# Two steps of the expert taken together from the 33rd step on, with a retuned table of orders

## The chip, the cores and the metric

The kernel runs on one core of one Trainium2 chip. The metric is the device time of one execution in microseconds (us); times of several executions are given by their median. The engines of the core are TensorE (PE in the rows, with PEld for its weight loads), VectorE (DVE), ScalarE (ACT), GpSimd (POOL) and SyncE (SP, which here issues all transfers).

## What is computed

Three parts follow each other, on 4 batches of 768 tokens, 8 heads of 48 values (d_model 384):

```python
# 1. attention with a decaying state, per head
for t in range(S):
    cur = einsum('bhd,bhe->bhde', u[None] * k[t], v[t])
    y[:, :, t] = einsum('bhd,bhde->bhe', r[t], state + cur)
    state = w[t][..., None] * state + einsum('bhd,bhe->bhde', k[t], v[t])
# 2. the first expert, x = y as [3072, 384]
h = x @ w_in                              # [3072, 2048]
g = h * clip(h + 3, 0, 6) / 6
x = g @ w_out                             # [3072, 384]
# 3. eight experts with four soft slots each
logits = x @ phi                          # [3072, 32]
d = softmax of logits over the tokens     # dispatch
slot_input = d.T @ x                      # [32, 384]
slot_out[e] = relu(slot_input[e] @ w1[e]) @ w2[e]
out = softmax of logits over the slots @ slot_out
```

w_in and w_out come as 64-bit floats and are turned into 32-bit ones in the kernel.

## The kernel before

The 3072 tokens are cut into 24 chunks g of 128 tokens (a batch has six), and three chunks make a block m of 384 tokens; there are eight blocks. The attention works chunk by chunk, the first expert block by block. One block goes through 16 steps of the expert, one for each 128 columns of w_in, so there are 128 steps s = 16 m + f in all.

One step is `moe_h` (L490): nine matmuls L498 (three pieces of d_model, each as three products of high and low parts) add up h of 384 tokens in a PSUM bank of the pool `ps_h`. The pool has NH = 3 banks, so the matmuls of step s + 3 can't start before step s has given its bank back. ScalarE's L501 computes the clipped part from the bank, VectorE's L502 multiplies it with the bank into the tile g (eight buffers); with L502 the bank is free. Two steps later `moe_t` (L521) turns g: for the middle blocks with VectorE's L529 and two transfers through memory (`moe_v`, L518 and L519), for the first two blocks and the end on TensorE (L222). `moe_l` multiplies four finished g with the product of w_out and phi (L551), which gives the logits. When a block's logits are complete, `r_logits` adds them up: ScalarE's L570 and VectorE's L571 split them into `part`, TensorE's L573 sums, and L583 to L646 make the running softmax and add the block into `acc` (L643, L646). After step 127 the tail does part 3.

For each chunk of the attention there are the loads (`wkr` L234, three buffers; `rkv` L243, two), the scan L250 on VectorE that makes `e` and ScalarE's small copy L254 of it, the second scan L260, the products L263 (with `e`, `pk`), L270 (`pq`), L276 (`rk`) and L280 (`ru`), each on VectorE or GpSimd by the tables PKD, PQD, RKD and RUD, the row sums L284, the diagonal of `att` (four of ScalarE's L293 or one of GpSimd's L295 by the table DGA, for two halves), the squares L267, the scores on TensorE (L306) and VectorE's masked copies L311 of them, the products L373 and L377, the copies L394 and L395 into y, and the state L333, L348, L349. A block's three y go through a transfer (L400), and ScalarE's L419 and GpSimd's or VectorE's L420 split them into the high and low part of x, which `moe_h` reads.

What sets the order: the program is a list of tokens (`seq`). A token is one of these pieces for one chunk, step or block (`pw19` the first scan of chunk 19, `h68` the matmuls, L501 and L502 of step 68, `o66` the turning of step 66). The start is written out by hand (START). After it each token of the attention has a step, worked out from its chunk's block (YB) and moved by the table LATER; at each step come first the tokens A, B, C (the splitting of w_in), then `h`, then the turning of two steps before, then the logits and then all other tokens of that step. The order of `seq` is the order of priority; a scheduler that simulates the engines makes each engine's order from it. Each engine then runs its instructions in that order, and an instruction that waits holds those behind it.

Of the kernel before, what the change touches and what calls it, by code (L numbers as in the profile page):

```python
# [29 lines left out]
NF = DFF // 128  # L30
# [134 lines left out]
def emit(ctx, tc, wkr, rkv, u, wi, wo, wot, phi, w1, w2, consts, out, flag=None, ysc=None):  # L165
    nc = tc.nc
    LAG = 2
# [735 lines left out]
    with ExitStack():  # L903
# [109 lines left out]
        seq = []  # L1013
# [54 lines left out]
        for s in sorted(set(steps) | set(range(NF * NB + LAG))):  # L1068
            early = [t for t in steps.get(s, ()) if t[0] in "ABC"]
            seq += early  # L1070
            if 0 <= s < NF * NB:
                seq.append(f"h{s}")
            late = [t for t in steps.get(s, ()) if t[0] not in "ABC"]
            if s >= LAG:
                seq.append(f"o{s - LAG}")
                if (s - LAG) % 4 == 3:
                    seq.append(f"v{(s - LAG) // 4}")
            seq += [t for t in late if t[0] == "l"]
            seq += [t for t in late if t[0] != "l"]
            if s == OPEN:  # L1080
                seq.append("open")
# [41 lines left out]
MT = 2  # L1123
QEND = 30
# [107 lines left out]
```

## Time and profile before

| | us |
|---|---|
| three executions, median | 535.35 (534.69 to 539.89) |
| the profiled execution | 535.26 |
| its span, first to last instruction | 533.5 |
| TensorE busy | 474.5 (89%) |
| VectorE busy | 366.4 (69%) |
| ScalarE busy | 237.5 (45%) |
| GpSimd busy | 153.0 (29%) |

The span is a little shorter than the execution, 1.8 us lie around it. The expert's matmuls L498 alone are 232.2 us of TensorE's work, L501 is 71.9 us of ScalarE's, L502 68.7 us of VectorE's. In a row of the order in time the number in front is the start, the next one the duration, both in us; in square brackets stands for how long the engine stood still just before the first instruction of the row, and what ended that. A row of several equal instructions (x9) runs from the first start to the last end.

### The profile page before, as it was taken

To read this page: it belongs to the slowest core of one execution; us is meant where nothing else is said; L and a number is where in the kernel's file an instruction comes from. 1 tells how busy PE (TensorE), PEld (TensorE's weight loads), DVE (VectorE), ACT (ScalarE), POOL (GpSimd) and SP (SyncE) were. 2 spreads that over 40 slices of the span, in tenths; PEclk is the share of its full clock that TensorE was granted. 3 is DMA by queue.
4 is the path that set the end of the run, shared out by engine and by line. 5 is a ranking of instruction groups with operands and counts; after the bars stand their busy time and mean duration, and the time that the engine had idled before them with its cause. 6 is when DMAs were issued, how large, how long until landed. Compare 5 with 4: busy or idle time off the path is not lost.

```text
span 533.5 us, 10165 instructions
## 1 busy us (share of the span) xinstructions
PE 474.5 (89%) x3934; PEld 375.0 (70%) x3934; DVE 366.4 (69%) x669; ACT 237.5 (45%) x580; POOL 153.0 (29%) x150
## 2 busy tenths in 40 slices
PE   5866786999999999999999997998999999989992
PEld 5755675688877688787875774886788788753462
DVE  5899999588425577798795799679667667442241
ACT  3574666477454343535362446245224323341021
POOL 3556932515101142233261643335130010000000
PEclk9687896698989999999999999999999999999995
DMA  8974235722303043668748965967496999977957
GB/s 297 413 280 123 88 122 183 259 86 70 107 3 109 1 121 109 184 192 279 268 120 249 326 224 145 286 222 197 119 329 199 377 315 336 419 324 270 398 172 232
DMA packets 40263, 114.13 MB, mean 214 GB/s; under 512 B 4464, under 2 KB 22928, under 8 KB 40208
## 3 DMA queue, kind: packets, MB, share of 16 engines
q1 hardware_dynamic: 40208, 113.41, 63.0%
q8 instruction: 33, 0.54, 0.4%
q14 instruction: 22, 0.18, 0.1%
HBM read 90.34 MB, written 22.02 MB: 211 GB/s over the span
## 4 chain that ended last, share of the span: by engine, by line
PE 45%; DVE 15%; DMA 9%; ACT 4%; issue 2%; POOL 2%; SPq 1%; POOLq 0%; DVEq 0%; ACTq 0%
PE h L498 22%; DMA rkv<-in_rkv_dram 4%; DMA wkr<-in_wkr_dram 4%; PE lps L551 3%; PE rot L222 3%; PE sides L643 3%; DVE g L502 2%; DVE wkr L260 2%; PE rot L799 2%; DVE e L250 2%; PE rot L373 2%; DVE gsq L529 2%; PE rot L377 2%; PE sides L306 1%; PE po L851 1%
## 5 line engine op out<-in xcount | busy, mean ns | idle before, releaser
L498 PE MATMUL h<-x,wt 128*128 128x384 f32 x1152 | 232.2, 349 | 21.6 <-DVE g L502 11.0
L498 PEld LDWEIGHTS h<-x,wt 128*128 128x128 f32 x1152 | 201.1, 192 | 43.6 <-DVE g L502 15.0
L501 ACT ACTIVATE g<-h,half 128x384 f32<-128x384 f32 x128 | 71.9, 575 | 62.6 <-PE h L498 57.7
L502 DVE SCALAR_TENSOR_TENSOR g<-g,h 128x384 f32<-128x384 f32 x128 | 68.7, 542 | 39.6 <-ACT g L501 36.0
L529 DVE STREAM_TRANSPOSE gsq<-g 128x384 f32<-128x384 f32 x88 | 49.6, 569 | 4.1 <-DMA via<-gsq 2.9
L250 DVE TENSOR_TENSOR_SCAN e<-wkr,d1r 128x516 f32<-128x516 f32 x24 | 32.3, 1351 | 23.2 <-DMA wkr<-in_wkr_dram 23.1
L295 POOL TENSOR_TENSOR att<-cst,cd 128x512 f32<-128x512 f32 x32 | 37.0, 1169 | 27.1 <-DVE cd L284 21.7
L270 POOL TENSOR_TENSOR wkr<-wkr 128x512 f32<-128x512 f32 x18 | 23.9, 1328 | 64.3 <-DVE wkr L260 35.9
L311 DVE COPY_PREDICATED att<-upm,sides 128x512 f32<-128x512 uint32 x48 | 32.1, 721 | 11.3 <-POOL att L295 5.7
L377 PE MATMUL rot<-att,rkv 128*64 128x128 f32 x384 | 32.5, 297 | 7.0 <-DVE att L311 7.0
L260 DVE TENSOR_TENSOR_SCAN wkr<-wkr,d1f 128x516 f32<-128x516 f32 x24 | 35.4, 1475 | 0.1
L377 PEld LDWEIGHTS rot<-att,rkv 128*64 128x64 f32 x384 | 25.0, 147 | 13.9 <-DVE att L311 8.2
L306 PE MATMUL sides<-wkr 64*128 64x128 f32 x384 | 31.6, 302 | 3.2 <-DVE wkr L270 1.2
L263 POOL TENSOR_TENSOR wkr<-wkr,e 128x512 f32<-128x512 f32 x16 | 20.9, 1309 | 44.2 <-DVE e L250 38.2
L306 PEld LDWEIGHTS sides<-wkr 64*128 64x128 f32 x384 | 26.0, 202 | 8.5 <-issue 4.3
L551 PE MATMUL lps<-g,ws 128*32 128x384 f32 x256 | 29.2, 519 | 1.2 <-DVE g L502 1.2
L293 ACT ACTIVATE att<-cst,cd 128x128 f32<-128x128 f32 x64 | 20.3, 393 | 16.5 <-DVE cd L284 16.5
L267 ACT ACTIVATE wkr<-wkr 128x516 f32<-128x516 f32 x24 | 15.2, 633 | 26.1 <-POOL wkr L270 15.6
L349 POOL TENSOR_TENSOR st<-sm,pt 128x192 f32<-128x192 f32 x20 | 13.8, 688 | 43.4 <-DVE sm L348 22.3
L280 POOL TENSOR_TENSOR rkv<-rkv,u_b 128x384 f32<-128x384 f32 x18 | 19.5, 1081 | 21.9 <-DVE rkv L276 9.2
L722 POOL COPY c<-chi 128x128 f32<-128x128 f32 x6 | 2.2, 364 | 78.7 <-DVE chi L720 40.9
L373 PE MATMUL rot<-wkr,st 64*64 64x128 f32 x320 | 24.5, 291 | 0.0
(156 smaller groups left out, 664.8 us busy)
## 6 DMA issues: line engine op xcount, KB each, us to landing
piece<-in_w_dram SPq DMA_DIRECT2D x24, 768.0 KB, 7.8
wkr<-in_wkr_dram SPq DMA_DIRECT2D x23, 770.0 KB, 5.2
via<-gsq SPq DMA_DIRECT2D x88, 192.0 KB, 4.4
gnat<-via SPq DMA_DIRECT2D x22, 768.0 KB, 5.9
rkv<-in_rkv_dram SPq DMA_DIRECT2D x24, 640.0 KB, 5.5
wi<-in_wi_dram SPq DMA_DIRECT2D x8, 768.0 KB, 8.9
wo<-in_wo_dram SPq DMA_DIRECT2D x8, 768.0 KB, 4.5
piece<-in_w_dram SPq DMA_DIRECT2D x8, 512.0 KB, 6.9
```

Source lines behind the costliest of these rows:

```text
L250: nc.vector.tensor_tensor_scan(out=flat(e)[:, ::-1], data0=behind.pop(g)[:, ::-1], data1=flat(d1r)[:, ::-1], initial=0.0, op0=ALU.mult, op ...
L260: nc.vector.tensor_tensor_scan(out=fw, data0=fw, data1=fd, initial=0.0, op0=ALU.mult, op1=ALU.add)
L295: nc.gpsimd.tensor_tensor(out=att[g][:, hs, :], in0=ident.unsqueeze(1).to_broadcast([128, 4, C]), in1=cd[g][:, hs].unsqueeze(2).to_broadca ...
L306: nc.tensor.matmul(out=sps[g][:, x, p * C:(p + 1) * C], lhsT=kt_[hs, p, :], rhs=qt_[hs, p, :])
L311: nc.vector.copy_predicated(out=att[g][:, x::2, :], mask=upm.unsqueeze(1).to_broadcast([128, NP, C]), data=ps[:, x].rearrange("p (a t) -> ...
L373: nc.tensor.matmul(out=ps[hs, k * C:(k + 1) * C], lhsT=stl[g][hs, p, :], rhs=qt_[hs, p, :], start=(k == 0), stop=False)
L377: nc.tensor.matmul(out=ps[64 * x:64 * x + 64, k * C:(k + 1) * C], lhsT=vt[:, 2 * p + x, :], rhs=a[:, 2 * p + x, :], start=(first and k == ...
L498: mm = nc.tensor.matmul(out=ps, lhsT=a[:, wp, f % 2, kt * 128:(kt + 1) * 128], rhs=x_[:, xp, kt, :], start=(kt == 0 and i == 0), stop=(kt ...
L501: ra = nc.scalar.activation(out=t, in_=ps, func=ACTF.Relu, scale=1.0 / 6.0, bias=half)
L502: sv = nc.vector.scalar_tensor_tensor(out=t, in0=t, scalar=1.0, in1=ps, op0=ALU.min, op1=ALU.mult)
L529: nc.vector.transpose(out=gsq[m, q][:, :, :, i, :].rearrange("p r j c -> p j r c"), in_=gt[s].rearrange("p (j r c) -> p j r c", j=n, r=4))
L551: mm = nc.tensor.matmul(out=lps[m][32 * i:32 * i + 32, :], lhsT=wsl[q][:, i, :], rhs=gt.pop(NF * m + 4 * q + i), start=(q == 0), stop=(q = ...
```

## The change

From step PAIR = 32 on, two steps are written one right behind the other: first the tokens A, B, C of both, then `h` of both, then for each of the two the turning, the logits and the other tokens. The tables are another set: RKD loses 0, 9 and 23 (to GpSimd), RUD gains 9, 10 and 14, PKD loses 17 and gains 21, PQD gains 11 (to VectorE), DGA gains a half of chunk 6 and one of chunk 19 (to ScalarE). YB puts the first chunk of block 0 one step earlier and the last chunks of blocks 6 and 7 one step later, the first pieces of w_in are loaded and split in another order (PLACES), START has another order, and about half of the numbers in LATER differ.

```diff
-        for s in sorted(set(steps) | set(range(NF * NB + LAG))):
-            early = [t for t in steps.get(s, ()) if t[0] in "ABC"]
-            seq += early
-            if 0 <= s < NF * NB:
-                seq.append(f"h{s}")
-            late = [t for t in steps.get(s, ()) if t[0] not in "ABC"]
-            if s >= LAG:
...
+        order = sorted(set(steps) | set(range(NF * NB + LAG)))
+        k = 0
+        while k < len(order):
+
+            both = order[k:k + 2] if order[k] >= PAIR and order[k] % 2 == 0 else order[k:k + 1]
+            k += len(both)
+            for s in both:
+                seq += [t for t in steps.get(s, ()) if t[0] in "ABC"]
+            seq += [f"h{s}" for s in both if 0 <= s < NF * NB]
+            for s in both:
+                late = [t for t in steps.get(s, ()) if t[0] not in "ABC"]
+                if s >= LAG:
+                    seq.append(f"o{s - LAG}")
+                    if (s - LAG) % 4 == 3:
+                        seq.append(f"v{(s - LAG) // 4}")
+                seq += [t for t in late if t[0] == "l"]
+                seq += [t for t in late if t[0] != "l"]
+                if s == OPEN:
+                    seq.append("open")
...
-RKD = (0, 2, 4, 7, 9, 10, 11, 12, 14, 16, 17, 19, 23)
-RUD = (4, 8, 12, 17, 18, 21)
-PKD = (2, 4, 8, 9, 10, 11, 12, 17)
-PQD = (0, 2, 3, 7, 13, 19)
+RKD = (2, 4, 7, 10, 11, 12, 14, 16, 17, 19)
+RUD = (4, 8, 9, 10, 12, 14, 17, 18, 21)
+PKD = (2, 4, 8, 9, 10, 11, 12, 21)
+PQD = (0, 2, 3, 7, 11, 13, 19)
...
 MT = 2
+PAIR = 32
...
-YB = ((-5, 3, 5), (0, 4, 8), (-6, -2, 4), (-7, -3, 2), (-6, -2, 2), (-10, -8, -1), (-13, -7, -4))
+YB = ((-6, 3, 5), (0, 4, 8), (-6, -2, 4), (-7, -3, 2), (-6, -2, 2), (-10, -8, -1), (-13, -7, -3))
...
-    'W2': 2, 'W3': 3, 'W1': 1, 'W0': 0, 'W4': 1, 'V0': 4, 'V1': 5, 'W5': 4, 'V2': 2, 'V3': 3, 'V4': 5, 'V5': 4, 'W6': 3, 'V6':
+    'W1': 1, 'W3': 3, 'W2': 2, 'W4': 1, 'W0': 0, 'V0': 4, 'V1': 5, 'W5': 4, 'V2': 2, 'V3': 3, 'V4': 5, 'V5': 4, 'W6': 3, 'V6':
```

What this does to an engine's order shows in the following rows. ScalarE before, from L501 of step 65 to that of step 68, where the logits of block 3 are split (`part`, L570); `pt` and `e` are chunk 19's and then chunk 20's:

```order
L501 ACTIVATE g_3081<-h_3071,half_95 128x384
L254 ACTIVATE pt_3126<-e_3123 128x4
L570 ACTIVATE part_3149<-lps_2694 128x384
L267 ACTIVATE e_3123,guard_96<-e_3123 128x516
L501 ACTIVATE g_3139<-h_3129,half_95 128x384
L501 ACTIVATE g_3174<-h_3164,half_95 128x384
L267 ACTIVATE wkr_3069,guard_96<-wkr_3069 128x516
L293 ACTIVATE att_3180<-cst0_91,cd_3146 128x128 x4
L395 ACTIVATE y_2763<-rot_3098 128x3x128
L254 ACTIVATE pt_3332<-e_3329 128x4
L267 ACTIVATE e_3329,guard_96<-e_3329 128x516
L501 ACTIVATE g_3231<-h_3221,half_95 128x384
```

The same place of the change, from `part` on; the three L501 are those of steps 66, 67 and 68:

```order
L570 ACTIVATE part_3165<-lps_2706 128x384
L501 ACTIVATE g_3146<-h_3136,half_95 128x384
L254 ACTIVATE pt_3133<-e_3130 128x4
L501 ACTIVATE g_3159<-h_3149,half_95 128x384
L267 ACTIVATE e_3130,guard_96<-e_3130 128x516
L501 ACTIVATE g_3227<-h_3217,half_95 128x384
L293 ACTIVATE att_3244<-cst0_91,cd_3050 128x128 x4
```

`part` now stands ahead of chunk 19's L254, and L501 of step 68 ahead of the four L293 instead of behind them and three more.

VectorE before, from L502 of step 67 to that of step 68:

```order
L502 SCALAR_TENSOR_TENSOR g_3174<-g_3174,h_3164 128x384
L394 COPY y3_2764<-rot_3098 128x128
L250 SCALAR_TENSOR_TENSOR e_3329<-wkr_3297,d1r_100 128x516
L583 TENSOR_REDUCE mx_3155<-rot_3148 128x1
L529 STREAM_TRANSPOSE gsq_3142<-g_3174 128x3x4x32
L252 RECIPROCAL d1f_99<-e_3329 128x4
L311 COPY_PREDICATED att_3180<-upm_92,sides_3186 128x4x128 x2
L585 TENSOR_TENSOR mrun_104<-mx_3155,mrun_104 128x1
L260 SCALAR_TENSOR_TENSOR wkr_3297<-wkr_3297,d1f_99 128x516
L276 TENSOR_TENSOR rkv_3178<-rkv_3178 128x384
L502 SCALAR_TENSOR_TENSOR g_3231<-g_3231,h_3221 128x384
```

VectorE in the change, from L502 of step 67 to that of step 68 and on to the first scan of chunk 20:

```order
L583 TENSOR_REDUCE mx_3171<-rot_3164 128x1
L502 SCALAR_TENSOR_TENSOR g_3159<-g_3159,h_3149 128x384
L284 TENSOR_REDUCE cd_3050<-rkv_3001 128x8
L270 TENSOR_TENSOR wkr_3048<-wkr_3048 128x512
L585 TENSOR_TENSOR mrun_104<-mx_3171,mrun_104 128x1
L529 STREAM_TRANSPOSE gsq_3162<-g_3159 128x3x4x32
L502 SCALAR_TENSOR_TENSOR g_3227<-g_3227,h_3217 128x384
L250 SCALAR_TENSOR_TENSOR e_3375<-wkr_3283,d1r_100 128x516
```

L502 of step 68 stands ahead of both scans of chunk 20, of the copies L311 and of L276; behind it they follow, mixed with L502 of steps 69 and 70.

ScalarE before around L501 of step 80, where x of block 6 is made (L419):

```order
L254 ACTIVATE pt_3772<-e_3769 128x4
L419 ACTIVATE x_3814<-y_3265 128x384
L254 ACTIVATE pt_3901<-e_3898 128x4
L419 ACTIVATE x_3814<-y_3265 128x384
L267 ACTIVATE e_3769,guard_96<-e_3769 128x516
L501 ACTIVATE g_3648<-h_3638,half_95 128x384
L419 ACTIVATE x_3814<-y_3265 128x384
L501 ACTIVATE g_3664<-h_3654,half_95 128x384
```

The same place of the change:

```order
L395 ACTIVATE y_3269<-rot_3597 128x3x128
L501 ACTIVATE g_3648<-h_3638,half_95 128x384
L419 ACTIVATE x_3857<-y_3269 128x384
L501 ACTIVATE g_3661<-h_3651,half_95 128x384
L419 ACTIVATE x_3857<-y_3269 128x384 x2
```

L501 of step 80 moved ahead of the first L419, that of step 81 ahead of the second and third.

## Rows read from the trace of the kernel before

**Rows 1.** Stretches (start:end): length, busy us of five engines, clock, DMA share, GB/s.
```profile
core 0: us, PE busy (x) PEld busy (x) DVE busy (x) ACT busy (x) POOL busy (x), PEclk, DMA share, GB/s
79.50:83.10 3.60, 0.04 (x1) 0.00 (x0) 3.60 (x5) 2.54 (x6) 0.22 (x1) 1.00 0.45 148
83.10:95.00 11.90, 10.26 (x51) 8.27 (x53) 9.60 (x11) 7.46 (x19) 3.78 (x2) 0.56 0.68 237
95.00:109.00 14.00, 12.73 (x100) 9.80 (x98) 9.08 (x14) 7.85 (x20) 7.45 (x7) 0.65 0.66 229
195.25:400.00 204.75, 193.13 (x1698) 153.60 (x1697) 158.85 (x309) 89.15 (x226) 75.21 (x74) 1.00 0.68 212
308.59:337.80 29.21, 25.04 (x200) 19.22 (x202) 29.11 (x54) 13.53 (x38) 11.27 (x11) 1.00 0.65 196
...
400.00:460.00 60.00, 60.00 (x401) 49.05 (x400) 40.88 (x96) 21.21 (x44) 2.96 (x10) 1.00 0.91 318
```

**Rows 2.** Waits of TensorE from 195 us on: total, times, longest.
```profile
PE h L498 <- DVE g L502: 5.4, 4, 2.5
```

**Rows 3.** TensorE in order of time, logits of block 3 and steps 65 to 71.
```profile
306.09 0.85 PE L551 MATMUL lps<-g,ws 128*32 128x384 f32 x8
...
311.35 0.44 PE L573 MATMUL rot<-part,sum 128*128 128x384 f32 x1 [1.08 <-ACT part L570]
...
316.18 4.80 PE L498 MATMUL h<-x,wt 128*128 128x384 f32 x26
...
324.29 1.86 PE L498 MATMUL h<-x,wt 128*128 128x384 f32 x9 [2.52 <-DVE g L502]
```

**Rows 4.** ScalarE in order of time, `part` and L501 of step 68.
```profile
310.83 0.47 ACT L570 ACTIVATE part<-lps 128x384 fp32r<-128x384 f32 x1
...
317.67 1.28 ACT L293 ACTIVATE att<-cst,cd 128x128 f32<-128x128 f32 x4 [0.20 <-DVE cd L284]
...
321.90 0.56 ACT L501 ACTIVATE g<-h,half 128x384 f32<-128x384 f32 x1
```

**Rows 5.** VectorE in order of time, scans of chunks 19 and 20, L502 of steps 68 and 74.
```profile
308.59 2.09 DVE L250 TENSOR_TENSOR_SCAN e<-wkr,d1r 128x516 f32<-128x516 f32 x1 [1.18 <-DMA wkr<-in_wkr_dram]
...
318.22 1.69 DVE L250 TENSOR_TENSOR_SCAN e<-wkr,d1r 128x516 f32<-128x516 f32 x1
...
323.69 0.54 DVE L502 SCALAR_TENSOR_TENSOR g<-g,h 128x384 f32<-128x384 f32 x1
...
340.11 0.56 DVE L502 SCALAR_TENSOR_TENSOR g<-g,h 128x384 f32<-128x384 f32 x1 [2.29 <-ACT g L501]
```

**Rows 6.** VectorE and GpSimd in order of time, products and second scans of chunks 17, 18.
```profile
290.34 0.66 DVE L263 TENSOR_TENSOR wkr<-wkr,e 128x512 f32<-128x512 f32 x1
290.92 1.23 DVE L260 TENSOR_TENSOR_SCAN wkr<-wkr,d1f 128x516 f32<-128x516 f32 x1
...
303.34 1.43 DVE L260 TENSOR_TENSOR_SCAN wkr<-wkr,d1f 128x516 f32<-128x516 f32 x1
...
302.50 1.19 POOL L263 TENSOR_TENSOR wkr<-wkr,e 128x512 f32<-128x512 f32 x1 [3.52 <-DVE e L250]
```

**Rows 7.** TensorE, then ScalarE, in order of time, steps 80 to 85.
```profile
364.96 1.86 PE L498 MATMUL h<-x,wt 128*128 128x384 f32 x9 [1.62 <-DVE g L502]
...
369.46 3.40 PE L498 MATMUL h<-x,wt 128*128 128x384 f32 x18 [0.70 <-DVE g L502]
...
361.73 0.53 ACT L419 ACTIVATE x<-y 128x384 fp32r<-128x384 f32 x1 [2.70 <-DMA y<-y]
...
363.29 0.56 ACT L501 ACTIVATE g<-h,half 128x384 f32<-128x384 f32 x1
```

**Rows 8.** TensorE, then GpSimd, in order of time, the first step of block 2.
```profile
196.18 2.56 PE L498 MATMUL h<-x,wt 128*128 128x384 f32 x13 [0.51 <-POOL x L420]
...
193.98 1.18 POOL L270 TENSOR_TENSOR wkr<-wkr 128x512 f32<-128x512 f32 x1 [5.06 <-DVE wkr L260]
```

**Rows 9.** TensorE in order of time, behind the last step.
```profile
472.24 0.52 PE L222 MATMUL rot<-cst,g 128*128 128x128 f32 x3 [0.88 <-DVE g L502]
472.69 0.85 PE L551 MATMUL lps<-g,ws 128*32 128x384 f32 x8
```

More of the change, by code (lines that the diff above doesn't have):

```diff
@@ L1067, in emit @@
             at_step(max(4 * z + 3 + LAG, list(PLACES).index(f"V{2 * z + 1}") + 1 if z < NQ else 0), f"l{z}")
-        for s in sorted(set(steps) | set(range(NF * NB + LAG))):
-            early = [t for t in steps.get(s, ()) if t[0] in "ABC"]
-            seq += early
-            if 0 <= s < NF * NB:
-                seq.append(f"h{s}")
-            late = [t for t in steps.get(s, ()) if t[0] not in "ABC"]
-            if s >= LAG:
[L1075 to L1081, printed above, removed]
+        order = sorted(set(steps) | set(range(NF * NB + LAG)))
[16 more added lines that the diff above has]
+                    seq.append("open")
         done, marks, queue = set(), {}, {}
@@ L1106 @@
 RB = 2
-RKD = (0, 2, 4, 7, 9, 10, 11, 12, 14, 16, 17, 19, 23)
-RUD = (4, 8, 12, 17, 18, 21)
-PKD = (2, 4, 8, 9, 10, 11, 12, 17)
-PQD = (0, 2, 3, 7, 13, 19)
+RKD = (2, 4, 7, 10, 11, 12, 14, 16, 17, 19)
+RUD = (4, 8, 9, 10, 12, 14, 17, 18, 21)
+PKD = (2, 4, 8, 9, 10, 11, 12, 21)
+PQD = (0, 2, 3, 7, 11, 13, 19)
 LOD = ()
 CUT = (0,)
-DGA = ((0, 0), (0, 1), (1, 1), (2, 0), (6, 1), (7, 0), (8, 0), (8, 1), (11, 1), (13, 1), (14, 1), (16, 1), (18, 0), (19, 0), (20, 0), (21, 0))
+DGA = ((0, 0), (0, 1), (1, 1), (2, 0), (6, 0), (6, 1), (7, 0), (8, 0), (8, 1), (11, 1), (13, 1), (14, 1), (16, 1), (18, 0), (19, 0), (19, 1), (20, 0), (21, 0))
 XP = (2, 4)
@@ L1168 @@
 START = """
-N0 cst wm0 L0 msk L1 N1 L2 W0 rk0 W1 phi N2 pw0 W2 pv0 ru1 ru0 pk0 W3 pw1 pq0 gp pk1 pc0 d00 d10 pv1 kt0 pq1 pw2 sm0 rk1 sc0
-sm1 rk2 y0 pc1 pv2 tm0 d01 yx0 pg0 pq2 pk2 tu0 d11 sc1 ru2 kt1 pc2 pg2 y1 tm1 pg1 tu1 d02 A0 B0 sm2 L3 kt2 yx1 d12 sc2 y2 tm2
-A1 B1 pw3 C0 A2 yx2 tu2 C1 B2 C2 N3 pv3
+N0 wm0 cst L0 L1 N1 L2 W0 W1 phi msk N2 rk0 pw0 pk0 pv0 pw1 ru0 W2 pq0 W3 ru1 pc0 gp rk1 pv1 d00 pk1 d10 kt0 sm0 sc0 y0 rk2
+pq1 pc1 pw2 sm1 yx0 pv2 pq2 pg0 tm0 pk2 d01 tu0 d11 ru2 pc2 sc1 kt1 pg2 y1 L3 tm1 sm2 tu1 d02 d12 A0 pg1 sc2 kt2 B0 yx1 tm2 y2
+A1 B1 yx2 pw3 C0 tu2 A2 C1 N3 pv3 B2 C2
 """.split()
```

52 rows, old and new, of the table LATER are left out of this document.

## The prediction

> **What bounds the kernel now.** The table of stretches comes first [rows 1]. From the 33rd step on, where the pairs begin (195.25 us), up to 400 us TensorE works 193.13 of 204.75 us: all that can be won there is 11.6 us of standing still. VectorE works 158.85 us of the same stretch, but from 308.59 to 337.80 us it works 29.11 of 29.21 us and TensorE 25.04; in this one place VectorE is the tight engine. The granted clock is 1.00 in all of it, so time won here is won at full speed. From 400 to 460 us TensorE never stops (60.00 of 60.00), so what is won before carries through to the tail. The view of waits comes second: from 195 us on the largest sum is the expert's matmul L498 waiting for VectorE's L502, 5.4 us in four waits, the longest 2.5 [rows 2]. The third view is the order in time of TensorE, ScalarE and VectorE around each of these waits; it says behind what the late L501 or L502 stood in its engine's queue.
>
> **What the change does, place by place.** On TensorE the order of before already has the steps together (26 matmuls of L498 in one run at 316.18) [rows 3], so pairing hardly moves TensorE. It moves ScalarE and VectorE: L501 and L502 of a pair come ahead of the attention's small operations instead of behind them, and the tables give a few of those to other engines.
>
> *Place A, the wait of 1.08 us at 311.35* [rows 3]. TensorE's L573 waits for ScalarE's `part` (L570), which ran 310.83 to 311.30 [rows 4]. It stood behind the activation on `e`, and that needs the scan L250 of chunk 19 on VectorE, 308.59 to 310.68, itself late by a load [rows 5]. Its own input, the logits, was ready at 306.94 (306.09 and 0.85) [rows 3]. After, `part` stands ahead of the activation on `e`. The wait goes: -1.1 us.
>
> *Place B, the wait of 2.52 us at 324.29* [rows 3]. Step 71 needs the bank that step 68 frees with L502. The matmuls of step 68 are the first eight of the run at 316.18 and end at about 317.7 (26 take 4.80, so 0.19 apart). ScalarE's L501 of step 68 starts only at 321.90: it stands behind four attention activations (317.67) and what follows them [rows 4]. VectorE's L502 stands behind the scan L250 of chunk 20 (318.22) and all that is between, and starts at 323.69 [rows 5]. After, L501 stands ahead of the four activations, and on VectorE only three small ones of what ran from 318.22 on are still ahead (about 1.2 us by the 0.54 of the L502 beside them). So L502 of step 68 ends at about 318.2 + 1.2 + 0.54 = 320 instead of 324.2, and earlier if VectorE uses its wait ahead of the scan of chunk 19 (1.18 us) for the L502, transpose and `part` that now stand in front of that scan, 318.8. TensorE without waits A and B would come to step 71 at 321.77 - 1.08 = 320.7. The wait of 2.52 us goes.
>
> The bound on A and B together is VectorE. In its busy stretch it stands still for nothing but those 1.18 us, and behind it for 2.29 us at 340.11, waiting for a late L501 [rows 5]: 3.5 us in all. A multiplication of chunk 21 comes to VectorE there (0.66 as the row at 290.34) [rows 6]. So no more than 3.5 - 0.7 = 2.8 us can be won, and some 0.3 more if the loads come earlier by place D. I count -3.1 for both, out of 3.6.
>
> *Place C, 1.62 us at 364.96 and 0.70 us at 369.46* [rows 7]. ScalarE's L501 of step 80 starts at 363.29 behind two casts of `x`, the first of which waited 2.70 us for a transfer until 361.73; on VectorE L502 of step 80 stood behind the scan L260 and two subtractions that need those casts. After, L501 of step 80 stands ahead of the first cast, and L502 ahead of the second scan of its chunk and of the subtractions, but behind the first scan of chunk 23, and so behind a load. I count -1.6 of the 2.3.
>
> *Place D, 0.51 us at 196.18* [rows 8]. GpSimd does a multiplication until 195.16 ahead of the subtractions for the next `x`. After, VectorE does it, and ahead of the L502 of step 29 that step 32 needs too. I count -0.2; the ends are -0.5 and +0.5.
>
> *Place E, the tail.* The transposes of the last step wait 0.88 us for L502, and the eight logit matmuls behind take 0.85 us [rows 9]. After, three of them stand ahead of that wait: about -0.3.
>
> *Multiplications that change engine.* Chunk 17's goes from VectorE (0.66) to GpSimd (1.19 as the row at 302.50) [rows 6]. Does VectorE win 0.66? The scan L260 took 1.43 us at 303.34 while GpSimd's multiplication ran until 303.69, and 1.23 at 290.92 with GpSimd idle: VectorE lost part of what GpSimd did beside it. The new place is just ahead of such a scan, so I count 0. The Trainium skill ("SBUF — State Buffer", section "Who interferes with whom") has a rule that speaks against the move: a VectorE instruction with two SBUF inputs and a GpSimd instruction that reads SBUF exclude each other, and the one that starts first holds up the other. By that rule nothing is won, without it 0.66; the trace's 1.43 against 1.23 agrees with it. No other swap stands where TensorE waits. Before step 32 the order of TensorE, SyncE and ScalarE is nearly row for row that of before; I count 0 there, 1.5 us either way.
>
> *New against it.* The two scans of chunk 21 and its multiplication now stand ahead of L502 of step 72 (priced above, by VectorE's bound); a scan of chunk 22 stands ahead of L502 of step 76, behind its load. Waits that a new order opens are in no trace of before. The waits from 195.25 to 400 us sum to 11.6; without A to D (1.08, 2.52, 2.32, 0.51) 5.2 are left, in pieces under 1.2. I put two new pieces of 0.45, +0.9 us; the ends are 0 and +5.2, as much again as there is.
>
> **The sum.** -3.1 - 1.6 - 0.2 - 0.3 + 0.9 = -4.3 us. The profiled execution took 535.26 us (its span 533.5), 0.09 under the median of 535.35. 535.26 - 4.3 is 531.0; **531.0 us** is the forecast.
>
> **The rivals.**
> (1) VectorE gives it back. For it: the 29.11 of 29.21 us, and the scans and copies that now stand behind a pair of L502 feed the attention of the next chunks, for whose results TensorE also waits. Against: over all of 195.25 to 400 us VectorE has 45.9 us of room [rows 1]. Then waits only move: A and B give 1.0, C 0.5, new ones take 1.5: 535.3.
> (2) The change doesn't do what it says: the steps stand together on TensorE already [rows 3], and the waits come back under other names. Same time as (1), so the two have one chance; 533 to 537.
> (3) It goes further: A, B, C, D whole, nothing new: 535.26 - 3.6 - 2.3 - 0.5 - 0.3 = 528.6, with up to 1.5 more from the start: 527 to 529.
> (4) Slower, by the clock. From 79.50 TensorE stood still (busy 0.04 of 3.60 us), and behind that the granted clock was 0.56 for 11.90 us and 0.65 for 14.00 us [rows 1]. 1.00 is the level of 2.4 GHz, 0.5 that of 1.2. TensorE was busy for 10.26 + 12.73 us there, at 1.00 that work is 10.26 x 0.56 + 12.73 x 0.65 = 14.0 us, so the low clock cost 9.0 us. If the new order of the start or of the weights' split opens one more such pause before 195 us, the time is 531.0 + 3.6 + 9.0 = 543.6. It decides where a pause as long as that one comes up; after the 2.52 us of place B the clock stayed at 1.00. For it: the order of the start, of the weights and of many small operations of the first chunks does change. Against: on TensorE, SyncE and ScalarE the rows there hardly differ.
>
> **Chances.** The forecast (529 to 533) 0.46, (1) and (2) together 0.27, (3) 0.17, (4) 0.10. The range leaves out (4) and the outer ends of (1) and (3): **527.0 to 537.5**; the likeliest one's own is 529 to 533. A difference of 1%, 5.35 us, is about what a measurement of this kernel can tell from no change. Faster by more than that, under 530.0: (3) and a third of the forecast, 0.32. Slower, over 540.7: (4), 0.10. Within: 0.58.
>
> **What would show it.** In the profile after: A is right if L573 no longer waits for `part`; B if no L498 between steps 64 and 76 waits over 1 us for L502 while VectorE stays without a break; C if step 83 follows without a wait of over 0.7 us; E if the last transposes wait about as before but fewer logit matmuls come behind. The forecast is wrong if VectorE's full stretch becomes longer and TensorE waits in it, if the clock from 195 to 460 us is below 1.00, or if TensorE stops between 400 and 460 us.

## The result, and the profile after

The changed kernel takes 543.38 us (median of 4, 540.52 to 544.12) beside 535.02 us for the kernel before in the same comparison (median of 4, 533.86 to 539.89). The ratio is 1.0124 with a 95% interval of 1.0082 to 1.0166: 1.2% slower, where 531.0 us and most likely no measurable difference were forecast. The ratios leave out executions in a slower state of the chip, so they need not equal the quotient of the medians. The profiled execution of the change has a span of 541.0 us, that of before 533.5.

Stretches of the profile of the change; the columns are those of [rows 1].

```profile
core 0: us, PE busy (x) PEld busy (x) DVE busy (x) ACT busy (x) POOL busy (x), PEclk, DMA share, GB/s
345.00:352.00 7.00, 4.45 (x43) 2.95 (x35) 1.79 (x3) 2.59 (x7) 3.04 (x3) 1.00 0.94 307
352.00:354.00 2.00, 0.00 (x0) 0.00 (x0) 1.97 (x4) 0.00 (x0) 1.57 (x2) 0.93 0.33 133
354.00:356.00 2.00, 0.81 (x3) 0.81 (x4) 2.00 (x4) 0.94 (x3) 2.00 (x2) 0.50 0.00 0
356.00:358.00 2.00, 2.00 (x8) 2.00 (x8) 2.00 (x5) 1.19 (x3) 1.10 (x2) 0.50 0.00 0
358.00:360.00 2.00, 2.00 (x16) 1.57 (x16) 2.00 (x5) 1.41 (x4) 0.72 (x1) 0.50 0.00 0
360.00:362.00 2.00, 2.00 (x29) 1.55 (x27) 0.85 (x3) 0.93 (x3) 0.32 (x1) 0.86 0.30 25
...
400.00:460.00 60.00, 59.82 (x418) 48.27 (x417) 39.58 (x89) 19.44 (x40) 4.84 (x11) 1.00 0.88 303
194.96:541.00 346.04, 318.22 (x2698) 242.81 (x2697) 224.19 (x460) 128.65 (x310) 75.61 (x84) 0.98 0.73 243
```

The same from the first matmul of step 32 to the end, kernel before:

```profile
195.25:533.50 338.25, 312.46 (x2700) 239.90 (x2698) 223.48 (x459) 127.71 (x307) 78.83 (x86) 0.98 0.75 248
```

Step 32 starts at 194.96 instead of 195.25 us, so in these two profiles everything is lost behind it. The last row of each view parts the loss: TensorE stands still for 346.04 - 318.22 = 27.8 us instead of 25.8, and is busy for 318.2 instead of 312.5. Not all of that busy time is work. At the low clock (0.50) a busy microsecond is counted as half a microsecond of work; taken over stretches of 1 us, the low clock costs the change 2.7 us (the four rows from 354 to 362) and before 1.2 (from 521 to 524 us, under the last output matmuls). Work at full clock is then 318.2 - 2.7 = 315.5 after and 312.5 - 1.2 = 311.3 before. **The loss of 7.8 us is 2.0 of standing still, 1.5 of low clock and 4.2 of TensorE's own work** (each rounded), for the same matmuls. Counting half is a little much (the nine matmuls at 355.19 below start 0.32 us apart, those at 320.29 0.18), so the costs of the low clock are upper ends. A second profile of each kernel (before_again and after_again below) gives 4.5 us for the work, but 0.9 instead of 2.0 for the standing still: the work is the part that comes back.

*Where it stands still.* TensorE in order of time, kernel after; the rows answer to [rows 3] and [rows 7]:

```profile
311.49 0.51 PE L573 MATMUL rot<-part,sum 128*128 128x384 f32 x2
...
325.01 1.86 PE L498 MATMUL h<-x,wt 128*128 128x384 f32 x9 [0.26 <-DVE g L502]
...
355.19 3.25 PE L498 MATMUL h<-x,wt 128*128 128x384 f32 x9 [5.01 <-DVE g L502]
...
372.23 3.83 PE L498 MATMUL h<-x,wt 128*128 128x384 f32 x18 [1.34 <-DVE g L502]
```

Places A and B are gone as forecast: L573 at 311.49 has no wait in front of it (1.08 us before), and step 71 starts at 320.29 without one (2.52 before; its row stands further below, behind a logit matmul). The 0.26 us at 325.01 are step 72's. But step 79, at 355.19, waits 5.01 us for L502 of step 76, the longest wait of this part of either profile, and its nine matmuls then take 3.25 us instead of 1.86, at a granted clock of 0.50. VectorE, kernel after, says what that L502 stood behind; the last row is ScalarE's, L501 of steps 76 and 77:

```profile
319.45 0.51 DVE L502 SCALAR_TENSOR_TENSOR g<-g,h 128x384 f32<-128x384 f32 x1
...
338.12 0.56 DVE L502 SCALAR_TENSOR_TENSOR g<-g,h 128x384 f32<-128x384 f32 x1
...
347.44 0.55 DVE L284 TENSOR_REDUCE cd<-rkv 128x8 f32<-128x384 f32 x1 [5.03 <-POOL rkv L280]
...
350.96 1.23 DVE L250 TENSOR_TENSOR_SCAN e<-wkr,d1r 128x516 f32<-128x516 f32 x1 [2.77 <-DMA wkr<-in_wkr_dram]
352.11 0.33 DVE L348 TENSOR_TENSOR sm<-st,rot 128x192 f32<-128x192 f32 x1
352.36 0.17 DVE L252 RECIPROCAL d1f<-e 128x4 f32<-128x4 f32 x1
352.56 2.12 DVE L260 TENSOR_TENSOR_SCAN wkr<-wkr,d1f 128x516 f32<-128x516 f32 x1
354.61 0.99 DVE L502 SCALAR_TENSOR_TENSOR g<-g,h 128x384 f32<-128x384 f32 x2
...
349.59 1.03 ACT L501 ACTIVATE g<-h,half 128x384 f32<-128x384 f32 x2
```

L502 of step 68 ends at 320.0 (324.2 before [rows 5]) and that of step 74 starts at 338.12 (340.11 before): up to there the change is 2 to 4 us ahead. Then both scans of chunk 22 stand ahead of L502 of step 76 (the x2 at 354.61 is steps 76 and 77), and the first waits 2.77 us for its load. In the kernel before both come behind it, and it starts at 349.76. L501 of step 76 ends at about 350.15 here (the two take 1.03), so by this estimate the load and the scans hold L502 up for 4.5 us. L501 is not early either: it stands behind ScalarE's L293, which waits for L284, and L284 waits 5.03 us for GpSimd's L280. The load is late because of SyncE. SyncE's issues, first before, then after (L234 is the load of chunk 22, L518 the first transfers of a turned block):

```profile
341.72 0.33 SPq L234 DMA_DIRECT2D wkr<-in_wkr_dram  x1
343.59 2.84 SPq L518 DMA_DIRECT2D via<-gsq  x4
```

```profile
341.19 2.71 SPq L518 DMA_DIRECT2D via<-gsq  x4
343.94 0.43 SPq L234 DMA_DIRECT2D wkr<-in_wkr_dram  x1
```

The load moved from ahead of the four transfers to behind them: it is issued 2.2 us later, and the scan that waits for it starts at 350.96, 7.0 us after the issue. The consumer went forward and its load went back.

*Where it works longer.* The four logit matmuls of one L551 group write four strips of 32 partitions of one bank. Each is two records, so a whole group reads x8. Kernel after, TensorE in order of time:

```profile
302.85 0.84 PE L551 MATMUL lps<-g,ws 128*32 128x384 f32 x4
303.62 0.45 PE L377 MATMUL rot<-att,rkv 128*64 128x128 f32 x4
...
319.52 0.83 PE L551 MATMUL lps<-g,ws 128*32 128x384 f32 x2
320.29 1.86 PE L498 MATMUL h<-x,wt 128*128 128x384 f32 x9
...
479.14 0.83 PE L551 MATMUL lps<-g,ws 128*32 128x384 f32 x2
479.90 0.87 PE L222 MATMUL rot<-cst,g 128*128 128x128 f32 x6
```

A row of x2 (one matmul) holds TensorE for 0.77 us until the next row starts, one of x4 for 0.77, a whole group of x8 for 0.78 (306.09 to 306.87 in the kernel before): four together take the time of one. The Trainium skill ("TensorEngine Tiling (Array Packing)", section "Key Properties") says that different tiles of the array can execute matmuls in parallel; the trace agrees, and shows the other side of it: a group that is cut pays once for each part. In the order of before one L551 group is cut in two behind step 32, in the change three are (2 + 2, the first row above and one at 306.24; 1 + 3, at 319.52 and 322.08; 3 + 1, whose last is the row at 479.14), and one L643 group, which works the same way, is cut too. TensorE's groups by line from 195 us on, first before, then after (busy us, mean ns):

```profile
L551 PE MATMUL lps<-g,ws 128*32 128x384 f32 x200 | 21.9, 497 | 1.2 <-DVE g L502 1.2
L643 PE MATMUL sides<-gnat,en 128*32 128x512 f32 x168 | 19.7, 596 | 0.0
```

```profile
L551 PE MATMUL lps<-g,ws 128*32 128x384 f32 x200 | 23.6, 497 | 0.5 <-DVE g L502 0.5
L643 PE MATMUL sides<-gnat,en 128*32 128x512 f32 x168 | 20.7, 597 | 0.1
```

The same counts and the same means, but 1.7 and 1.0 us more: 2.7 of the 4.2. L306 and L377 show 0.5 more each, where their runs are cut too. Counted as the work above, with each instruction taken until the next one starts, L377 and L222's transposes of `wkr` are 0.6 us more each and L306 and L373 0.4 each; the other lines together are 0.4 less.

### The profile page after: what moved, and what is told of

Its sections match the earlier page's. It is cut to its first block, busy times and chain, and to the rows that moved or that the text cites. A ratio compares the mean times of both kernels' runs of the same rounds, so it can differ in the third digit from the quotient of the medians.

```text
span 541.0 us, 10149 instructions
## 1 busy us (share of the span) xinstructions
PE 477.9 (88%) x3934; PEld 374.3 (69%) x3934; DVE 367.6 (68%) x670; ACT 239.6 (44%) x588; POOL 150.1 (28%) x147
## 4 chain that ended last, share of the span: by engine, by line
PE 43%; DMA 22%; DVE 20%; ACT 5%; issue 4%; POOL 2%; SPq 2%; DVEq 0%; POOLq 0%; ACTq 0%
PE h L498 17%; DMA wkr<-in_wkr_dram 9%; DMA rkv<-in_rkv_dram 6%; PE rot L222 4%; DMA via<-gsq 3%; PE rot L377 3%; DVE wkr L260 3%; PE lps L551 3%; DVE g L502 2%; DVE gsq L529 2%; PE sides L306 2%; PE sides L643 2%; DVE e L250 2%; PE rot L799 2%; PE rot L373 2%
## 5 line engine op out<-in xcount | busy, mean ns | idle before, releaser
L501 ACT ACTIVATE g<-h,half 128x384 f32<-128x384 f32 x128 | 72.1, 576 | 72.5 <-PE h L498 69.1
L502 DVE SCALAR_TENSOR_TENSOR g<-g,h 128x384 f32<-128x384 f32 x128 | 68.5, 540 | 37.7 <-ACT g L501 34.3
L250 DVE TENSOR_TENSOR_SCAN e<-wkr,d1r 128x516 f32<-128x516 f32 x24 | 31.2, 1302 | 28.1 <-DMA wkr<-in_wkr_dram 28.0
L295 POOL TENSOR_TENSOR att<-cst,cd 128x512 f32<-128x512 f32 x30 | 35.0, 1181 | 29.1 <-DVE cd L284 29.1
L377 PE MATMUL rot<-att,rkv 128*64 128x128 f32 x384 | 32.7, 293 | 6.8 <-DVE att L311 6.8
L311 DVE COPY_PREDICATED att<-upm,sides 128x512 f32<-128x512 uint32 x48 | 32.2, 720 | 8.6 <-POOL att L295 3.8
L260 DVE TENSOR_TENSOR_SCAN wkr<-wkr,d1f 128x516 f32<-128x516 f32 x24 | 37.5, 1562 | 0.2
L270 POOL TENSOR_TENSOR wkr<-wkr 128x512 f32<-128x512 f32 x17 | 21.9, 1286 | 54.7 <-DVE wkr L260 33.6
L263 POOL TENSOR_TENSOR wkr<-wkr,e 128x512 f32<-128x512 f32 x16 | 20.2, 1261 | 58.7 <-DVE e L250 54.0
L306 PE MATMUL sides<-wkr 64*128 64x128 f32 x384 | 31.9, 300 | 3.5 <-DVE acc L646 2.3
L377 PEld LDWEIGHTS rot<-att,rkv 128*64 128x64 f32 x384 | 24.7, 143 | 14.5 <-DVE att L311 7.9
L306 PEld LDWEIGHTS sides<-wkr 64*128 64x128 f32 x384 | 26.0, 199 | 9.5 <-issue 3.7
L551 PE MATMUL lps<-g,ws 128*32 128x384 f32 x256 | 30.6, 516 | 1.2 <-ACT ws L486 0.6
L293 ACT ACTIVATE att<-cst,cd 128x128 f32<-128x128 f32 x72 | 22.6, 394 | 19.1 <-DVE cd L284 19.0
L222 PE MATMUL rot<-cst,g 128*128 128x128 f32 x120 | 21.2, 295 | 4.3 <-ACT ws L486 2.5
L373 PE MATMUL rot<-wkr,st 64*64 64x128 f32 x320 | 24.4, 286 | 0.5 <-ACT ws L486 0.5
```

Source lines behind the costliest of these rows:

```text
L222: return nc.tensor.transpose(out=out, in_=in_, identity=ident)
L250: nc.vector.tensor_tensor_scan(out=flat(e)[:, ::-1], data0=behind.pop(g)[:, ::-1], data1=flat(d1r)[:, ::-1], initial=0.0, op0=ALU.mult, op ...
L260: nc.vector.tensor_tensor_scan(out=fw, data0=fw, data1=fd, initial=0.0, op0=ALU.mult, op1=ALU.add)
L295: nc.gpsimd.tensor_tensor(out=att[g][:, hs, :], in0=ident.unsqueeze(1).to_broadcast([128, 4, C]), in1=cd[g][:, hs].unsqueeze(2).to_broadca ...
L306: nc.tensor.matmul(out=sps[g][:, x, p * C:(p + 1) * C], lhsT=kt_[hs, p, :], rhs=qt_[hs, p, :])
L373: nc.tensor.matmul(out=ps[hs, k * C:(k + 1) * C], lhsT=stl[g][hs, p, :], rhs=qt_[hs, p, :], start=(k == 0), stop=False)
```

## The experiments

Theory P: the order in one place (load 22 behind the transfers, scans of chunk 22 ahead of L502) makes the loss. Rivals: the pairs or the tables as such cost, wherever the waits fall; or TensorE's cut groups do. Each comparison has its own runs of the kernel before: 535.85 us for the first four experiments (19 runs), 533.75 for the next four (23), 536.15 for the last three (13). Length, idle, clock and work are counted as above, from step 32 to the end.

**Load 22 issued ahead of the four transfers again (load_first).**

```diff
-    'Q18': -5, 'L22': -2, 'rk15': 2,
+    'Q18': -5, 'L22': -4, 'rk15': 2,
-PIN = {'L5': 'h1', 'L6': 'h0'}
+PIN = {'L5': 'h1', 'L6': 'h0', 'v18': 'L22'}
```

LATER brings the load two steps forward. The entry added to PIN, called a pin from here on, holds its first token behind its second: here the transfers `v18` behind the load (for which the function of the load returns its instruction).

> The changed kernel with one order changed on SyncE: the load of wkr of chunk 22 goes ahead of the four transfers via of steps 72 to 75 instead of behind them (a pin, and its place in the list two steps earlier). The scan L250 of chunk 22 stays ahead of L502 of step 76. Theory 1 (the scan waits for a load that is held up on SyncE, TensorE stops behind it for 5.0 us and runs at a lower clock for some 6 us after it): the load is issued at about 340.5 instead of 343.9 and lands before 347.5, so the wait of TensorE of 5.0 us falls under 1.5 us, the clock stays at 1.00, and the time is 534 to 537.5 us. Theory 2 (pairing overloads VectorE, the load only shows where): 541 us or more. Theory 3 (the new start and order of the weights): 541 us or more.

541.15 us (539.37 to 542.95, 4 runs), ratio 1.0111 (1.0029 to 1.0192). The time lies in the range of theories 2 and 3, not in theory 1's 534 to 537.5, and the wait did not fall under 1.5 us. SyncE, then TensorE and ScalarE of this kernel:

```profile
343.23 0.33 SPq L234 DMA_DIRECT2D wkr<-in_wkr_dram  x1
344.03 2.99 SPq L518 DMA_DIRECT2D via<-gsq  x4
```

```profile
354.13 1.84 PE L498 MATMUL h<-x,wt 128*128 128x384 f32 x9 [2.29 <-DVE g L502]
...
350.60 1.28 ACT L293 ACTIVATE att<-cst,cd 128x128 f32<-128x128 f32 x4 [7.32 <-DVE cd L284]
351.79 0.56 ACT L501 ACTIVATE g<-h,half 128x384 f32<-128x384 f32 x1
```

The order of SyncE is that of before again, the scan no longer waits for the load, and the wait is 2.29 us instead of 5.01. The unchanged kernel had 3.30 in its second profile (after_again below), so the load's part is 1.0 to 2.7 us. The clock stays high here (nine matmuls in 1.84 us). The rest is not the scans' alone: L501 of step 76 ends at 352.35 and L502 starts at 353.55, so the scans still hold it up by 1.2 us; L501 itself stands behind L293, which waits for GpSimd's L280 by way of L284. But the total hardly follows: elsewhere TensorE waits 2.38 us for L646, at 291.02, and this time the clock falls behind that wait and costs 3.4 us. In the change itself nearly the same wait (2.27 us at 290.18) left the clock at full speed.

**First scan of chunk 22 held behind step 77 (scan_behind).**

```diff
-PIN = {'L5': 'h1', 'L6': 'h0'}
+PIN = {'L5': 'h1', 'L6': 'h0', 'pw22': 'h77'}
```

> The changed kernel with one order changed on VectorE: the scan L250 of chunk 22 stands behind L502 of steps 76 and 77 instead of ahead of them (a pin). The load stays behind the four transfers. Theory 1: TensorE's wait of 5.0 us for L502 goes, since L502 of step 76 no longer waits for the load; the attention of chunk 22 comes late as before but has room; the clock stays at 1.00 from 195 to 460 us; 533 to 537 us. Theory 2: 541 or more. Theory 3: 541 or more.

543.26 us (536.07 to 544.1, 4 runs), ratio 1.0107 (1.0000 to 1.0214): theory 1's 533 to 537 us missed again. VectorE of this kernel, L502 of steps 76 and 77:

```profile
353.80 1.02 DVE L502 SCALAR_TENSOR_TENSOR g<-g,h 128x384 f32<-128x384 f32 x2 [1.73 <-ACT g L501]
```

The wait of 5.01 us became 1.68 (354.41). What is left has no scan and no load of chunk 22 in it: VectorE stands ready and waits for L501, which stands behind L293 as above. Other waits came up: 0.98 at 367.41 and 2.01 at 372.04. A low clock behind a wait of 2.52 us for L646, at 292.22, cost 3.2 us. So the scan does stand in the way, but moving it alone doesn't pay.

**The tables without the pairs (no_pairs), the pairs without the tables (pairs_alone).** The first is the change, the second the kernel before with the new loop and PAIR.

```diff
-PAIR = 32
+PAIR = 999
```

```diff
+PAIR = 32
```

> The changed kernel with PAIR = 999, so steps are taken one by one as before, with all the new tables. In the order that comes out, the load of chunk 22 is ahead of the four transfers on SyncE, and the scan of chunk 22 still ahead of L502 of step 76. Theory 1: a small wait there, under 1.5 us, and no low clock: 534 to 538 us. Theory 2 (pairing is what costs): the waits of before come back, 535 us. Theory 3 (the new start costs): 541 us or more.

> The kernel before with the pairing alone, all tables old. In the order that comes out, the load of chunk 22 is behind the four transfers, as in the changed kernel, but its scan is behind L502 of step 79. Theory 1: no wait of 5 us, the waits of 2.5 us at step 71 and 1.1 us at part are gone as in the changed kernel: 531 to 534.5 us. Theory 2 (pairing overloads VectorE): 541 us or more. Theory 3: 535 us.

no_pairs: 537.84 us (533.78 to 540.55, 10 runs), ratio 1.0058 (1.0020 to 1.0095). pairs_alone: 541.67 us (535.81 to 543.0, 10 runs), ratio 1.0122 (1.0068 to 1.0175). Pairing alone costs as much as the whole change; the tables alone cost about half of that. no_pairs lies in theory 1's range, pairs_alone far outside it and in theory 2's. Theory P doesn't hold as it stands: in pairs_alone the scans of chunk 22 stand behind L502 of step 76, and the loss is the same. Their parts differ:

| | length | idle | low clock | work |
|---|---|---|---|---|
| before | 338.25 | 25.8 | 1.2 | 311.3 |
| no_pairs | 338.0 | 24.1 | 0.1 | 313.8 |
| pairs_alone | 343.1 | 29.6 | 0.1 | 313.5 |
| the change | 346.0 | 27.8 | 2.7 | 315.5 |

In work the two halves nearly add up (4.7 beside 4.2 us): the tables bring 2.5 us (the L643 cut is in no_pairs, not in pairs_alone), the pairs 2.2 (three L551 cuts instead of one: taken until the next row, L551 is 21.9 us instead of 20.2). Idle time comes with the pairs. Where the load of chunk 22 stands on SyncE does too; no_pairs, then pairs_alone:

```profile
340.58 0.33 SPq L234 DMA_DIRECT2D wkr<-in_wkr_dram  x1
342.32 2.67 SPq L518 DMA_DIRECT2D via<-gsq  x4
```

```profile
342.99 2.04 SPq L518 DMA_DIRECT2D via<-gsq  x4
345.08 1.13 SPq L234 DMA_DIRECT2D wkr<-in_wkr_dram  x1
```

In no_pairs the scans of chunk 22 stand ahead of L502 of step 76 as in the change, yet no matmul waits for it: the load comes ahead, the second scan takes 1.23 us instead of 2.12, and L502 starts at 350.02. In pairs_alone the waits are at other places, all within 25 us:

```profile
350.94 0.65 PE L222 MATMUL rot<-cst,wkr 128*128 128x128 f32 x4 [1.84 <-DVE sm L348]
...
366.87 1.85 PE L498 MATMUL h<-x,wt 128*128 128x384 f32 x9 [2.07 <-DVE g L502]
...
371.49 1.83 PE L498 MATMUL h<-x,wt 128*128 128x384 f32 x9 [1.65 <-DVE g L502]
```

In the two kernels with pairs VectorE's L284 waits 5.0 and 5.7 us for GpSimd's L280 of chunk 20, in the two without them 2.9 and 2.7. Counted from step 32, L284 starts 1.2 us (the change) and 1.6 us (pairs_alone) later than before, and what stands behind it comes later too. In the change, as in the kernel before, GpSimd's L276 ahead of L280 waits for another load, `rkv` (until 345.33, before 344.40); in pairs_alone it waits for TensorE's L306.

**Three faults of the change mended together (after_pins)**, and **the waits of before moved with the same kind of pins (before_pins).**

```diff
-PIN = {'L5': 'h1', 'L6': 'h0'}
+PIN = {'L5': 'h1', 'L6': 'h0', 'pw17': 'ra2', 'pw22': 'h77', 'v18': 'L22'}
```

```diff
-PIN = {'L5': 'h1', 'L6': 'h0'}
+PIN = {'L5': 'h1', 'L6': 'h0', 'pw17': 'ra2', 'pw20': 'h68', 'ax6': 'h80'}
```

`pw17` behind `ra2` lets the update L646 of block 2 go ahead of the first scan of chunk 17, `pw22` and `v18` are the two pins above (with L22 at -4). In before_pins `pw20` holds the first scan of chunk 20 behind step 68 and `ax6` the casts of block 6 behind step 80: the waits of places B and C; `pw17` is for the wait of 0.98 us for L646 at 290.39.

> The changed kernel with three orders held: the update of acc ahead of the first scan of chunk 17 on VectorE (TensorE's wait of 2.3 to 2.5 us at about 290 goes), the load of chunk 22 ahead of the four transfers of steps 72 to 75 on SyncE, and the scan of chunk 22 behind L502 of steps 76 and 77. Theory A (the loss is made of L502 and acc standing behind scans that wait for loads, and of the low clock behind waits of TensorE of 2.4 us and more): no wait over 1.5 us between 195 and 470 us, the clock 1.00 in all of it, 533 to 537 us. Theory B (pairing itself costs, wherever the waits fall): 539 us or more.

> The kernel before, steps one by one, with three orders held: the update of acc ahead of the first scan of chunk 17, the first scan of chunk 20 behind L502 of step 68, and the casts and subtractions for x of block 6 behind L501 and L502 of step 80. Theory A: the waits of 1.0, 2.5 and 1.6 us go and little comes in their place, 530.5 to 533.5 us. The rival (VectorE and the loads give it back: what stands behind comes later and other waits open): 535 to 537 us.

after_pins: 539.07 us (536.62 to 541.47, 4 runs), ratio 1.0117 (1.0051 to 1.0182); length 339.7, of it idle 23.4, low clock 3.4, work 312.9. The time lies at the edge of theory B, not in theory A's 533 to 537. The waits became fewer, but two that are left (3.06 us at 294.63 for ScalarE's L322, 2.24 at 367.28) were each followed by a low clock, 1.7 us each. before_pins: 536.5 us (531.64 to 541.61, 12 runs), ratio 1.0043 (1.0005 to 1.0081). Theory A's gain did not come: such pins do not win what the waits show. The waits went to other places: 1.78 us at 313.23 for L311, 2.04 at 364.75, 1.89 at 368.96.

**Pairs only behind the attention (pairs_from_96), and before once more.**

```diff
+PAIR = 96
```

> The kernel before with all its tables, and pairs only from step 96 on, where the attention's scans are done. Theory A: no scan and no load is left to get in front of a pair, so 534.5 to 536.5 us, as before. Theory B (pairing itself costs): 537 us or more.

> The kernel before once more, unchanged, for a second profile. The waits of TensorE after 195 us should come at the same instructions with the same lengths within 0.4 us; what may differ is the clock and the first 195 us. 533 to 540 us.

pairs_from_96: 534.09 us (530.84 to 540.8, 10 runs), ratio 1.0007 (0.9966 to 1.0047). Where no pieces of the attention are left, pairs neither gain nor cost, as far as the interval tells. before_again (no edit, one execution) took 539.88 us: length 339.9, idle 25.5, low clock 3.4, work 311.1. Its idle time and work are those of the first profile; the rest of its lag is low clock, behind waits of 2.04 us at 272.31 and 1.95 at 315.41, and 3 us lost before step 32. The single waits did not come back within the 0.4 us expected: the one of place B is 1.01 us here instead of 2.52, that for `part` 1.95 instead of 1.08. So work can be compared from profile to profile, the sum of idle time within 1.4 us (after_again below), and a single wait not; the low clock is different in each execution.

**Eight L551 groups of before cut in 2 + 2 (split_groups).** This gives the cut a price of its own. In `moe_l` (and a new token `k` for the second half, two steps later):

```diff
+            if z in SPLIT and i < 2: continue
...
+SPLIT = (20, 21, 22, 24, 25, 26, 28, 29)
```

> The kernel before with eight of the groups of four logit matmuls (L551; groups 20, 21, 22, 24, 25, 26, 28 and 29) cut into two and two, the second two behind the matmuls of two steps later. Up to step 86 TensorE's order is that of before, and no matmul is added. If a part of a group takes TensorE as long as the whole (the four write different quarters of the partitions and run side by side; the rows of before have 0.78 us for a group), eight more parts cost 8 x 0.78 = 6.2 us and the time is 540 to 543 us. If a matmul costs the same wherever it stands, 534 to 536.5 us.

544.85 us (541.94 to 546.82, 4 runs), ratio 1.0147 (1.0067 to 1.0227): slower than before by as much as the change, with nothing but cuts (540 to 543 us were expected from them, 534 to 536.5 without a price). Its groups by line (L552 is L551 here, L559 the cut second halves):

```profile
L552 PE MATMUL lps<-g,ws 128*32 128x384 f32 x176 | 22.5, 497 | 0.8 <-DVE g L502 0.7
...
L559 PE MATMUL lps<-g,ws 128*32 128x384 f32 x32 | 7.5, 498 | 0.0
```

The first parts take no less time for being half as large (0.77 us). The second halves hold TensorE 6.2 us until the next row, in eight parts of 0.76 to 0.77: one half is itself cut in two, another starts together with a whole group. Work rises from 311.3 to 318.2, by 6.9.

**The change with the pins and with fewer cuts (after_best), and the change once more.** As after_pins, with

```diff
-    'l16': 6, 'rk14': 1,
+    'l16': 6, 'l15': 1, 'rk14': 1,
...
-    'ra4': 2, 'pg11': 1,
+    'ra4': 6, 'pg11': 1,
...
+PIN = {'L5': 'h1', 'L6': 'h0', 'l15': 'h66', 'l16': 'h71', 'l30': 'h127', 'ra4': 'h91', 'pw17': 'ra2', 'pw22': 'h77', 'v18': 'L22'}
```

> The changed kernel with acc ahead of the first scan of chunk 17, the load of chunk 22 ahead of the four transfers, the scan of chunk 22 behind L502 of step 77 as in after_pins, and besides with the logits of groups 15, 16 and 30 and the products with en of block 4 (L643) behind a step each, so that only two of their groups are cut where the changed kernel cuts three and one. Theory A with the cut groups: 1.5 to 2.5 us less than after_pins, 535 to 538 us. If pairing costs something else besides: no better than after_pins, 538.5 or more.

> The changed kernel once more, unchanged, for a second profile. If the wait of 5.0 us in front of step 79 comes from the order on SyncE and VectorE, it is there again within 0.7 us, with L502 of step 76 behind the scan that waits for the load; whether the clock falls behind it or behind the wait of 2.3 us at 290 us can differ. 540 to 544 us.

after_best: 538.85 us (533.5 to 540.55, 10 runs), ratio 1.0048 (0.9999 to 1.0098); length 338.7, idle 23.4, low clock 3.1, work 312.2. One L551 group is cut, no L643 (19.7 us as in before); but L306 now stands in 20 runs instead of 15 and takes 1.7 us more. By its profile, work fell by 3.3 us and idle time by 4.4 against the change. The ratio fell from 1.0124 to 1.0048: more than half of the loss by these figures, but the two intervals overlap, so the share isn't fixed. Nor is it better than after_pins by the 1.5 to 2.5 us of theory A: 538.85 us lies in the other theory's range. It is about level with before; no version beat it. after_again (no edit, one execution): 542.86 us, length 344.1, idle 26.4, low clock 2.0, work 315.6. The long wait is there again with the load behind the four transfers, but with 3.30 us at 356.48 it lies outside the 0.7 us expected: the scan waited 1.06 us for the load, not 2.77. A low clock followed again.

## Why the prediction was wrong

**Places A and B: right.** L573 no longer waits for `part`; between steps 64 and 76 the longest wait for L502 is 0.26 us; L502 of step 68 came 4.2 us earlier (as forecast), and step 71 at 320.29 (320.7 were forecast). Up to step 76 the gain holds: its matmuls start at 336.77 instead of 341.61. That the two waits were worth 3.6 us was read from one execution; in before_again they are 1.95 and 1.01.

**New against it: the step that failed first, by the order in time.** The prediction named the cause ("a scan of chunk 22 stands ahead of L502 of step 76, behind its load") and priced it with 0.45 us, half of 0.9. It cost 5.01 us of waiting and 2.7 of low clock. The waits that stood elsewhere in the trace were no measure for this one; VectorE's rows around the new place are. A scan, its wait for a load, a reciprocal, a second scan and the small copy L348 are 1.23 + 2.77 + 0.17 + 2.12 + 0.33 = 6.6 us ahead of an L502 on which a bank hangs. The upper end of +5.2 us was near it by luck: it was the sum of all waits left, not worked out from this place. In the second profile the wait was 3.30 us. Also missing was SyncE: the prediction speaks of its order before step 32 only, and the load that had moved behind four transfers made 1.0 to 2.7 us of the wait (load_first beside the two profiles of the change).

**Place C: the letter right, the gain not.** Step 83 follows without a wait. Step 84 waits 1.34 us (372.23) for L502 of step 81 instead. Of the 2.3 us of before 1.5 are left, a gain of 0.8 where 1.6 were forecast (in the second profiles 0.8 of 2.8 are left). ScalarE, kernel after:

```profile
368.38 0.53 ACT L419 ACTIVATE x<-y 128x384 fp32r<-128x384 f32 x1 [3.14 <-DMA y<-y]
368.81 0.56 ACT L501 ACTIVATE g<-h,half 128x384 f32<-128x384 f32 x1
```

L501 of step 81 stands behind the first cast, which waits for a transfer that SyncE now issues at 362.67 instead of 356.37. The wait moved by one step with the transfer, as rival (1) had it for all places.

**"Pairing hardly moves TensorE": wrong, and the largest term.** The sum has no term for TensorE's own work, so it stood at nothing. The steps did stand together, but what stands between them was cut: +4.2 us of work, with cuts of L551 and L643 for 2.7 of it. The same in the second profiles of both kernels (315.6 against 311.1). split_groups shows the price, 0.76 to 0.77 us a part.

**Place E: the sign named for it did not show.** The last transposes have no wait in front of them (0.88 before), but what fills it is one logit matmul cut off a group (479.14, 0.76 us), and the whole last group still comes behind, at 480.71. The gain is about 0.1 us, where 0.3 were forecast.

**Place D and the multiplications: right.** Step 32 runs without a wait inside it in both profiles of the change (0.51 us before). That it starts 0.3 us earlier shows nothing: its start differs by 2.9 us between the two profiles of before. The multiplication of chunk 17 went to GpSimd, and VectorE won next to nothing, as forecast; kernel after, the place of [rows 6]:

```profile
290.25 1.64 DVE L260 TENSOR_TENSOR_SCAN wkr<-wkr,d1f 128x516 f32<-128x516 f32 x1
...
289.62 1.18 POOL L263 TENSOR_TENSOR wkr<-wkr,e 128x512 f32<-128x512 f32 x1 [6.36 <-DVE e L250]
```

The scan ends at 291.89; before it ended at 292.15 behind the multiplication, and VectorE had started its scan L250 0.2 us later there. So of the 0.66 us some 0.06 are won. Other rows say the same; kernel after, VectorE's second scan, then GpSimd at the time of the scan at 352.56:

```profile
333.36 1.22 DVE L260 TENSOR_TENSOR_SCAN wkr<-wkr,d1f 128x516 f32<-128x516 f32 x1
```

```profile
352.43 1.17 POOL L263 TENSOR_TENSOR wkr<-wkr,e 128x512 f32<-128x512 f32 x1 [3.25 <-DVE e L250]
353.56 1.43 POOL L349 TENSOR_TENSOR st<-sm,pt 128x192 f32<-128x192 f32 x1
```

With GpSimd idle the scan takes 1.22 us, beside these two it took 2.12. The one that starts later pays: in no_pairs the scan starts first (348.87) and takes 1.23 us, and GpSimd's L263 beside it (349.05) takes 2.03 instead of 1.17.

**The clock: right as a mechanism, wrong in place and size.** Rival (4) expected a low clock behind a pause in the start, 3.6 + 9.0 us. It came in the wait that ends at 355.19, 5.0 + 2.7 us, in the stretch where the prediction saw 1.00 throughout. The argument that the clock held after 2.52 us in place B doesn't carry: a wait of 2.52 us in scan_behind was followed by the low clock. That (4)'s 543.6 us lies beside the measured 543.38 is luck: the pause it spoke of, in the start, did not come.

**What stays open.** Why the attention's pieces around chunk 20 run later with pairs wasn't followed to its end: no run moved the load of `rkv`, or L280, alone. Of the 2.5 us that work is higher in no_pairs the cut of L643 is 1.1 and L306 and L377 0.7 each; why their runs come out so isn't known. No run took away the cuts and nothing else, so their share of the 1.2% rests on the count of work and on split_groups. What part of the 1.2% is low clock can't be fixed by one profile: it was 2.7 us in one execution of the change and 2.0 in another, 1.2 and 3.4 in two of before.

## What to carry to other kernels

Matmuls that fill the array side by side must stay together in the order: compare their groups in the order before and after a change, and charge each cut the time of a whole group. Compare two profiles of the unchanged kernel before pricing a wait: one that was 2.52 us in the first was 1.01 in the second. When an instruction moves forward past one that frees a bank, add up everything that comes with it in its queue, and look where its load stands among the transfers that wait. A wait that is removed is worth its microseconds only when the next wait in line, and the clock behind it, stay as they were.

## What the runs showed of the hardware that was not expected

One logit matmul alone holds TensorE as long as four side by side: 0.76 to 0.78 us. Of TensorE's waits behind step 32 and before 470 us in the thirteen profiles, 21 lasted 1.89 us or more; behind 12 of these the granted clock stood at 0.50 (1.2 GHz instead of 2.4) for 3 to 7 us, at a price of 1.6 to 3.4 us each, counted as above; behind 8 it stayed at 1.00, and one came while it was low. The same length is found on both sides (2.52 us). None of the eleven waits from 1.5 to 1.84 us was followed by it. This is one way in which executions of one kernel come to differ (530 to 543 us for the kernel before over all its executions): between its two profiles the low clock differs by 2.2 us, and the start up to step 32 by 2.9.
